# Attention feeding a gated layer on one core: fewer small attention matmuls, one batch's masks added elsewhere, and another order of the first phase

## The chip, the cores and the metric

One core of a Trainium2 chip runs the whole program. The core has five engines with queues of their own: TensorE (PE, with its weight loads shown as PEld), VectorE (DVE), ScalarE (ACT), GpSimd (POOL) and SyncE (SP, which issues the transfers). The metric is the device time of one execution in microseconds; less is better.

## What is computed

```python
scores = scale * np.matmul(q, k.transpose(0, 1, 3, 2))          # 8 batches, 8 heads, 576 x 64
mask_local = (rel >= 0) & (rel < 32)                            # heads 0 to 3
mask_strided = (rel >= 0) & (pos[None, :] % 32 == pos[:, None] % 32)   # heads 4 to 7
scores = np.where(masks[None, :, :, :], scores, -1000000000.0)
attn = softmax(scores)                                          # written out in full, 1e-09 in the sum
x = (attn @ v) as 4608 tokens x 512
out = (sigmoid(x @ w_gate) * (x @ w_val)) @ w_out               # 512 -> 1536 -> 512
```

All in 32-bit floats. The large products are made with the operands split in a rounded part and a remainder, three matmuls of 128x512 for each product.

## The kernel before

**Attention.** A batch has four *pairs* of heads: 0 and 2 are local, 1 and 3 are strided. A local pair works in 18 blocks of 32 queries, which see 64 keys each; a strided pair in 11 groups of 54 (three classes of the stride, 18 tokens each). One pair goes through these steps, named by letters in the order table: Q and V load, S makes the scores in PSUM (`score`), F0 adds the mask (`mask`), F1 takes the maximum, F2 or F3 subtracts it on VectorE or GpSimd, E is the exponential on ScalarE, N0 to N4 the sum, its reciprocal and the multiplication, T transposes the probabilities on TensorE and P copies them out of PSUM on ScalarE (in batches 3 to 7 VectorE transposes them instead, steps B), X multiplies by the values (`weigh`), H, L and R split the result. So `S32` is the scores of batch 3, pair 2.

`score` places the blocks in slots of 128 rows: four local blocks or two strided groups fill a slot, so 20 local and 12 strided places are computed for 18 and 11 blocks; the rest repeats the first blocks and is not used. Each place takes two matmuls (one for each head of the pair). In the batches of `BY_MASK` (0, 1 and 2) the mask is not added by VectorE: two matmuls of an identity with the mask (`masks`, 128x320 or 128x324) put it in PSUM first, and the scores accumulate onto it. F0 is then not there, and F1 and F2 read PSUM.

`weigh` takes the probabilities of a block from one half of the 128 rows (64 rows each, r = 0 or 1) and has 36 matmuls for a local pair. In batches 3 to 7 two blocks follow each other in one half, then two in the other; the last two blocks, 16 and 17, are both in half 0.

**The layer.** The first phase works on batch 0 alone: twelve chunks of the hidden dimension, each with its weights loaded as raw words (W), put together and split by ScalarE, VectorE and GpSimd (a, b, w, k, u, l, U, D), twelve matmuls for the gate and twelve for the value (g), and twelve for the output (O). The other batches follow in four steps of two batches (the last of one) with a scheme of seven products for a 2x2 block matrix; these matmuls are the lines 637.

**The order.** Nothing is scheduled by a planner: the table `ORDERS` lists all steps, one string for each part of the program, and each engine gets its instructions in that order. `|` is the next product of the current part. Engines run their queues in order, and wait on semaphores for what they read and for buffers to come free. The tiles in PSUM that the first phase's attention uses are few: `BANKS` gives them, and T of pair 1 and S of pair 3 in batch 0 have the same one (`"T01": "o0"`, `"S03": "o0"`).

Of the kernel before, what the change touches and what calls it, by code (L numbers as in the profile page):

```python
# [20 lines left out]
P = 128  # L21
# [3 lines left out]
LB = 32  # L25
# [21 lines left out]
BY_MASK = (0, 1, 2)  # L47
# [35 lines left out]
C Q00 Z00 W0.0 i0 a0.0 d4 Z01 b0.0 S00 F100 W0.1 F200 w0.0 p0.0 d7 E00 a0.1 Q01 N000 b0.1 S01 N100 W1.0 u0.0 N400 Q02  # L83
a1.0 N300 d1 T00 w0.1 p0.1 l0.0 F101 U0.1 F201 P00 E01 b1.0 V00 w1.0 S02 X00 Z02 R00 H00 N001 W0.2 N101 F102 a0.2 N401
F202 L00 W1.1 p1.0 V01 E02 N301 D0.1 d3 T01 b0.2 a1.1 g0.1.0 W2.1 N002 P01 U1.0 g0.0.0 l1.0 Q03 b1.1 X01 N102 S03 w1.1
N402 N302 W2.0 H01 a2.0 L01 p1.1 U1.1 Z03 T02 R01 F103 V02 g0.0.1 g0.1.1 F203 P02 b2.0 E03 g1.0.0 W2.2 w2.0 a2.1 X02
D1.1 g1.0.1 N003 N103 H02 p2.0 g1.1.0 u2.0 N403 N303 V03 w0.2 g1.1.1 T03 L02 Q11 W3.0 a2.2 g1.1.2 b2.2 g0.0.2 W1.2
k0.2 b2.1 R02 P03 Z30 w2.1 U0.2 X03 g1.0.2 w2.2 p2.1 D0.2 H03 g0.1.2 L03 a3.0 h0 b3.0 w3.0 R03 U2.1 a1.2 b1.2 g0.0.3
D2.0 g1.1.3 w1.2 s0 k1.2 k2.2 Z11 S11 W3.1 i1 u1.2 g0.1.3 k3.0 m0 W4.0 a4.0 g1.0.3 Q10 F111 g2.0 U2.2 U3.0 s1 F211 V11
l2.1 W4.1 h1 x0 h2 y0 W3.2 Z10 S10 m1 D1.2 E11 g2.1 l2.2 a3.1 K0 N011 N111 b3.1 D3.0 F110 O0 Z20 s2 a3.2 b4.0 N411 x1  # L90
N311 F210 T11 z0 w3.1 k3.1 y1 g3.0 V10 b3.2 m2 z2 Q12 w3.2 Q13 U3.1 E10 k3.2 l3.1 P11 W4.2 X11 U3.2 x2 w4.0 R11 N010
N110 h3 H11 O1 W5.1 S13 W5.0 a4.1 b4.1 Z13 N410 D3.2 k4.0 z1 w4.1 s3 N210 W5.2 k4.1 a4.2 y2 Z12 u4.0 F113 b4.2 U4.1
F213 a5.0 g3.1 T10 D4.0 b5.0 w4.2 a5.1 b5.1 k4.2 g4.0 P10 l4.1 U4.2 w5.0 m3 z3 S12 W6.0 O2 k5.0 l4.2 h4 E13 w5.1 s4
U5.0 a5.2 x3 b5.2 l5.0 F112 F212 X10 W6.1 w5.2 E12 Q21 k5.2 k5.1 a6.1 y3 R10 u5.2 W6.2 W7.0 g4.1 b6.1 w6.1 N012 h5 H10
# [1239 lines left out]
```

## Time and profile before

| what | value |
|---|---|
| time, median of 3 runs | 894.06 us (893.12 to 899.36) |
| the profiled execution | 893.55 us |
| its span, first to last instruction | 891.8 us |
| TensorE busy, share | 883.2 us, 99% |
| VectorE, ScalarE, GpSimd busy | 648.6, 473.3, 324.0 us |
| granted clock of TensorE | 1.000 |

A timeline lists merged instructions with start and length in us, the tiles they write and read, and the count. One fp32 matmul of the program leaves two records in the trace, one with rounded operands leaves one. TensorE's instructions overlap, so the cost of a block is read from its start to the next block's start.

### The profile page before, as it was taken

Reading aid. Unit: us, or ns where it says so; the run is one execution under the profiler, and the core shown is the slowest. Engines: PE = TensorE matmul, PEld = TensorE weight load, DVE = VectorE, ACT = ScalarE, POOL = GpSimd, SP = SyncE. Lnnn points to the kernel's source line nnn. Section 1 sums busy time; section 2 is a strip of 40 time slices with the busy share of each in tenths; the row PEclk is TensorE's granted clock in tenths of the full one; section 3 lists DMA queues with packets and bytes.
Section 4 is the critical chain, followed back from the end, with each engine's and each line's share of the span. In section 5 each row is a group of like instructions: output and inputs, shape, how many; then the busy total and the mean of one; then the engine's idle time right before and its main releaser. Section 6 shows DMA issues by size and latency. Waiting matters only on the chain.

```text
span 891.8 us, 18880 instructions
## 1 busy us (share of the span) xinstructions
PE 883.2 (99%) x7522; PEld 724.2 (81%) x7522; DVE 648.6 (73%) x993; ACT 473.3 (53%) x870; POOL 324.0 (36%) x259
## 2 busy tenths in 40 slices
PE   8999999999999999999999999999999999999997
PEld 6788888888888787888888888888888888888886
DVE  5898878999689999764789997233689852233874
ACT  5798767865566554544355535332646443233542
POOL 5553556965331575100034441001326420001194
PEclk9999999999999999999999999999999999999999
DMA  9998685895786799865536779775256896551577
GB/s 358 337 349 289 234 265 203 292 411 172 322 354 198 260 273 320 320 258 223 212 104 218 242 251 294 277 274 205 100 188 205 247 317 251 216 198 48 173 203 167
DMA packets 106120, 219.08 MB, mean 246 GB/s; under 512 B 44721, under 2 KB 64305, under 8 KB 99889
## 3 DMA queue, kind: packets, MB, share of 16 engines
q1 hardware_dynamic: 101712, 216.83, 70.5%
q10 hardware_dynamic: 4320, 1.05, 0.6%
q8 instruction: 59, 0.97, 0.4%
q14 instruction: 29, 0.23, 0.1%
HBM read 169.62 MB, written 48.23 MB: 244 GB/s over the span
## 4 chain that ended last, share of the span: by engine, by line
PE 91%; DVE 5%; DMA 1%; issue 1%; ACT 0%; POOL 0%; ACTq 0%; SPq 0%; DVEq 0%; POOLq 0%
PE sum L637 51%; PE g__2109 L637 11%; PE v__2110 L637 11%; PE sum L689 4%; PE v L637 4%; PE g L637 4%; PE s L382 3%; PE x L487 2%; DVE pt L457 1%; DMA qk<-in_qk_l 1%; PE t L444 1%; PE sum L487 1%; PE gv L637 1%; DVE stage L962 0%; DVE mx L424 0%
## 5 line engine op out<-in xcount | busy, mean ns | idle before, releaser
L637 PE MATMUL sum<-stage 128*128 128x512 f32 (+1 forms) x720 | 164.9, 386 | 0.7 <-ACT early_base L1044 0.7
L962 POOL TENSOR_TENSOR stage<-h,stage 128x512 fp32r<-128x512 f32 x67 | 100.0, 1514 | 180.2 <-ACT stage L960 148.9
L637 PEld LDWEIGHTS sum<-stage 128*128 128x128 f32 x720 | 132.0, 188 | 28.1 <-ACT early_base L1044 0.9
L960 ACT CAST stage<-h 128x512 fp32r<-128x512 f32 x168 | 97.5, 621 | 104.9 <-PE sum L637 30.8
L637 PE MATMUL sum<-x,mix 128*128 128x512 f32 x576 | 135.7, 390 | 0.2 <-ACT gq L837 0.2
L637 PEld LDWEIGHTS sum<-x,mix 128*128 128x128 f32 x576 | 107.8, 188 | 23.2 <-ACT gq L837 0.7
L457 DVE STREAM_TRANSPOSE pt<-sb 32x320 f32<-32x320 f32 (+1 forms) x160 | 85.7, 536 | 7.2 <-PE x L487 3.7
L825 DVE TENSOR_TENSOR s<-sum,gp 128x512 f32<-128x512 f32 x48 | 32.9, 688 | 74.4 <-PE sum L637 72.0
L962 DVE TENSOR_TENSOR stage<-h,stage 128x512 fp32r<-128x512 f32 x101 | 78.4, 800 | 8.3 <-ACT stage L960 6.8
L637 PE MATMUL sum<-x1h,mix 128*128 128x512 f32 x192 | 63.7, 391 | 0.0
L637 PE MATMUL sum<-x3h,mix 128*128 128x512 f32 x192 | 63.6, 391 | 0.0
L637 PE MATMUL sum<-x6h,mix 128*128 128x512 f32 x192 | 63.4, 390 | 0.0
L826 DVE TENSOR_TENSOR h<-s 128x512 f32<-128x512 f32 x48 | 35.4, 742 | 37.8 <-ACT s L827 37.4
L837 ACT COPY gq<-sum 128x512 f32<-128x512 f32 x48 | 28.1, 588 | 44.6 <-PE sum L637 44.5
L967 POOL TENSOR_TENSOR h<-h 128x512 f32<-128x512 f32 x13 | 18.7, 1436 | 86.2 <-DVE h L826 82.2
L827 ACT ACTIVATE s<-sum 128x512 f32<-128x512 f32 x24 | 14.3, 596 | 67.2 <-PE sum L637 67.2
L436 POOL TENSOR_TENSOR sb<-sb,mx 128x640 f32<-128x640 f32 (+1 forms) x15 | 20.8, 1390 | 75.0 <-DVE mx L432 67.5
L827 ACT ACTIVATE s<-s 128x512 f32<-128x512 f32 x48 | 30.0, 633 | 27.2 <-DVE s L825 27.2
L637 PEld LDWEIGHTS sum<-x3h,mix 128*128 128x128 f32 x192 | 36.0, 188 | 7.7
L637 PEld LDWEIGHTS sum<-x1h,mix 128*128 128x128 f32 x192 | 36.0, 188 | 7.7
L637 PEld LDWEIGHTS sum<-x6h,mix 128*128 128x128 f32 x192 | 36.0, 188 | 7.5
L825 DVE TENSOR_TENSOR s<-sum,gq 128x512 f32<-128x512 f32 x48 | 32.6, 685 | 10.8 <-PE sum L637 6.5
(237 smaller groups left out, 1947.8 us busy)
## 6 DMA issues: line engine op xcount, KB each, us to landing
mix<-mix SPq DMA_DIRECT2D x36, 1024.0 KB, 8.6
mix<-mix SPq DMA_DIRECT2D x36, 768.0 KB, 7.0
stage<-sums_out SPq DMA_DIRECT2D x96, 256.0 KB, 4.3
mix<-mix SPq DMA_DIRECT2D x12, 1792.0 KB, 8.4
stage<-outer SPq DMA_DIRECT2D x72, 256.0 KB, 4.1
vv<-in_v_l SPq DMA_DIRECT2D x16, 640.0 KB, 6.1
qk<-in_qk_l SPq DMA_DIRECT2D x16, 592.0 KB, 5.7
out<-turned_P SPq DMA_DIRECT2D x50, 128.0 KB, 4.0
```

The source lines that it names most:

```text
L382: nc.tensor.matmul(sc[g * m : (g + 1) * m, j * BANK + s * kk : j * BANK + (s + 1) * kk], qk[d, q0 : q0 + m], qk[d, k0 : k0 + kk], start=no ...
L436: engine.tensor_tensor(prob, prob, by_row, op=ALU.mult)
L457: nc.vector.transpose(dst[to : to + LB, :, col : col + LB], src[rows : rows + LB, :, h * LB : (h + 1) * LB])
L487: nc.tensor.matmul(halves[r][j * D : (j + 1) * D, (u * per + g) * m : (u * per + g + 1) * m], v[rows, (u * per + g) * P + j * D : (u * per ...
L637: nc.tensor.matmul(o, w, x, start=first and n == 0, stop=last and n == len(todo) - 1, skip_group_check=onto)
L689: nc.tensor.matmul(o, a[:, i * P : (i + 1) * P], b, start=first and n == 0, stop=last and n == 2)
L825: add = lambda to, x, y: nc.vector.tensor_tensor(to, x, y, op=ALU.add)
L826: mul = lambda to, x, y: nc.vector.tensor_tensor(to, x, y, op=ALU.mult)
L827: sig = lambda to, x: nc.scalar.activation(to, x, AF.Sigmoid)
L837: P6=(g2, v2, dict(P6=lambda: nc.scalar.copy(new("gq"), g2)), dict(P6=lambda: nc.scalar.copy(new("vq"), v2)), False),
L960: nc.scalar.copy(h, src)
L962: engine.tensor_tensor(l, src, h.bitcast(F32), op=ALU.subtract)
```

## The change

The scores of the batches in `BY_MASK` leave out the places that no block needs. Batch 2 leaves `BY_MASK`: its masks are added by VectorE, and its padded places stay. In local pairs of batches 3 to 7 block 17 goes to half 1 of the rows, in the scores, in the values' layout (made on the host, a zero block put ahead of it) and in `weigh`; the copy of the last 64 tokens then reads two pieces of 32 columns. `ORDERS` is written anew up to the first third of its second string.

```diff
-BY_MASK = (0, 1, 2)
+BY_MASK = (0, 1)
...
+        apart_last = local and b >= BY_PE
...
-            for n in range(ns * (P // m)):
+            blocks = NBL if local else NG
+            for n in range(blocks if by_mask else ns * (P // m)):
                 s, g = divmod(n, P // m)
-                q = n % (NBL if local else NG)
+                q = n % blocks
+                if apart_last and s == ns - 1:
+                    g = (g % 2) * 2 + g // 2
...
                 u, r = divmod(s, 2)
+                if apart_last and n == NBL - 1:
+                    r, g = 1, 0
...
-                left = [(halves[0][:, full : full + REST], lambda x: x)]
+                if not apart_last:
+                    left = [(halves[0][:, full : full + REST], lambda x: x)]
+                elif apart:
+                    left = [(halves[r][:, full : full + LB], lambda x, r=r: x[:, r * LB : (r + 1) * LB]) for r in range(2)]
+                else:
+                    src = xp.rearrange("p (r n) -> p r n", r=2)[:, :, full : full + LB]
+                    left = [(src, lambda x: x.rearrange("p (r n) -> p r n", r=2))]
...
-C Q00 Z00 W0.0 i0 a0.0 d4 Z01 b0.0 S00 F100 W0.1 F200 w0.0 p0.0 d7 E00 a0.1 Q01 N000 b0.1 S01 N100 W1.0 u0.0 N400 Q02
+Z01 C d4 Q00 i0 W0.0 a0.0 S00 b0.0 Z00 W0.1 F100 F200 w0.0 E00 N000 Z02 d7 a0.1 Q01 b0.1 S01 p0.0 u0.0 N100 N400 W1.0
...
```

What the new order does is seen on the engines. The lines of the changed kernel stand some 2 to 13 further down: its L370, L387, L449 and L453, L494, L650 and L702 are L368 (masks), L382 (scores), L444 and L448 (T), L487 (`weigh`), L637 and L689 (the layer's products) of before; its L402 and L406 are L397 and L401 (F0), L413 is L408 (F1), L421 is L416 (F2).

TensorE in batch 0, before, from the scores of pair 2 (`s_2`) on; `t_1` is T of pair 1, `x_1` its output, `v_0` and `g_0` the first chunk's products:

```order
L368 MATMUL s_2_261<-rounded 128x320 x2
L382 MATMUL s_2_261<-qk_2_234 32x64 x40
L487 MATMUL x_0_304<-pt_0_253,vv_0_258 64x32 x36
L680 MATMUL zeros_out<-zeros 128x256 x3
L444 MATMUL t_1_364<-cst,first_x_134 128x128 x6
L637 MATMUL v_0_373<-x_0_108,w_231 128x512 x3
L637 MATMUL g_0_383<-x_0_108,w_231 128x512 x3
L487 MATMUL x_1_390<-first_x_135 64x54 x22
L368 MATMUL s_3_414<-rounded 128x324 x2
L382 MATMUL s_3_414<-first_x_134 64x54 x24
L444 MATMUL t_2_455<-cst,sb_2_341 128x128 x4
L448 MATMUL t_2_455<-cst,sb_2_341 64x64 x2
```

The same place after the change:

```order
L370 MATMUL s_2_249<-rounded 128x320 x2
L387 MATMUL s_2_249<-qk_2_231 32x64 x36
L494 MATMUL x_0_300<-pt_0_245,vv_0_288 64x32 x36
L693 MATMUL zeros_out<-zeros 128x256 x3
L449 MATMUL t_1_356<-cst,first_x_115 128x128 x6
L650 MATMUL v_0_374<-x_0_108,w_224 128x512 x3
L370 MATMUL s_3_385<-rounded 128x324 x2
L387 MATMUL s_3_385<-first_x_115 64x54 x22
L494 MATMUL x_1_410<-first_x_116 64x54 x22
L449 MATMUL t_2_438<-cst,sb_2_184 128x128 x4
L453 MATMUL t_2_438<-cst,sb_2_184 64x64 x2
L650 MATMUL g_0_458<-x_0_108,w_224 128x512 x3
```

The masks and scores of pair 3 (`s_3`) now stand ahead of `x_1` and right behind the first three products; the second three (`g_0`) come behind `t_2`.

ScalarE beside it, before: the copies of `t_1` out of PSUM are the two L465, and L591 and L595 take the upper and lower words of a raw weight tile:

```order
L595 ACTIVATE first_x2h<-first_x0h 128x512
L535 COPY xr_117<-x_0_304 128x64
L527 CAST x_0_108<-x_0_304 128x512
L591 ACTIVATE first_x3l<-first_x1h 128x512
L420 ACTIVATE sb_2_341<-sb_2_341 128x640
L595 ACTIVATE first_x3l<-first_x1h 128x512
L591 ACTIVATE first_x3h<-first_x0l 128x512
L465 COPY first_x_135<-t_1_364 128x512
L465 COPY first_x_135<-t_1_364 128x256
L595 ACTIVATE first_x3h<-first_x0l 128x512
L527 CAST x_2_110<-x_1_390 128x16x18
```

After the change (L548 is the copy of the rest, L540 the rounding, L604, L608, L425 and L470 are L591, L595, L420 and L465):

```order
L608 ACTIVATE first_x2h<-first_x0h 128x512
L604 ACTIVATE first_x3l<-first_x1h 128x512
L548 COPY xr_114<-x_0_300 128x64
L540 CAST x_0_108<-x_0_300 128x512
L608 ACTIVATE first_x3l<-first_x1h 128x512
L604 ACTIVATE first_x3h<-first_x0l 128x512
L425 ACTIVATE sb_2_184<-sb_2_184 128x640
L608 ACTIVATE first_x3h<-first_x0l 128x512
L470 COPY first_x_116<-t_1_356 128x512
L470 COPY first_x_116<-t_1_356 128x256
L540 CAST x_2_110<-x_1_410 128x16x18
```

One L604 went ahead of the copy of `x_0`, and one L608 more stands ahead of the copies of `t_1`.

TensorE in batch 2, before, from the masks of pair 1 to the transposes of pair 0:

```order
L368 MATMUL s_1_1430<-rounded 128x324 x2
L382 MATMUL s_1_1430<-first_x_134 64x54 x24
L637 MATMUL v_7_1461<-x_0_108,w_1282 128x512 x3
L637 MATMUL v_7_1461<-x_1_109,w_1282 128x512 x3
L637 MATMUL v_7_1461<-x_2_110,w_1282 128x512 x3
L637 MATMUL v_7_1461<-x_3_111,w_1282 128x512 x3
L689 MATMUL sum_783<-w_1060,first_x6l 128x512 x3
L689 MATMUL sum_784<-w_1060,first_x6l 128x512 x3
L689 MATMUL sum_785<-w_1060,first_x6l 128x512 x3
L689 MATMUL sum_786<-w_1060,first_x6l 128x512 x3
L444 MATMUL t_0_1491<-cst,sb_0_801 128x128 x4
L448 MATMUL t_0_1491<-cst,sb_0_801 64x64 x2
```

After the change:

```order
L387 MATMUL s_1_1397<-first_x_115 64x54 x24
L650 MATMUL v_7_1424<-x_0_108,w_1326 128x512 x3
L650 MATMUL v_7_1424<-x_1_109,w_1326 128x512 x3
L650 MATMUL v_7_1424<-x_2_110,w_1326 128x512 x3
L650 MATMUL v_7_1424<-x_3_111,w_1326 128x512 x3
L449 MATMUL t_0_1454<-cst,sb_0_455 128x128 x4
L453 MATMUL t_0_1454<-cst,sb_0_455 64x64 x2
```

The masks are gone, and the transposes of pair 0 (`t_0`) come 12 products after the scores of pair 1, where there were 24.

## Rows read from the trace of the kernel before

**Rows 1.** Page, part 1: busy time of each engine, share of the span, instructions.

```profile
PE 883.2 (99%) x7522; PEld 724.2 (81%) x7522; DVE 648.6 (73%) x993; ACT 473.3 (53%) x870; POOL 324.0 (36%) x259
```

**Rows 2.** Waits of PE: who waited for whom, us in total, times, longest.

```profile
PE s L368 <- ACT pt L467: 0.8, 1, 0.8
...
PE t L444 <- POOL first_x L436: 0.5, 1, 0.5
PE s L382 <- DMA qk<-in_qk_l: 0.5, 1, 0.5
```

**Rows 3.** Timeline of PE, masks and scores: start, us, line, tiles, records.

```profile
84.96 0.46 PE L368 MATMUL s<-rounded 128*128 128x320 f32 x2
85.35 1.04 PE L382 MATMUL s<-qk 64*32 64x64 f32 x80
86.32 3.06 PE L637 MATMUL g<-x,w 128*128 128x512 f32 x12
...
155.02 0.39 PE L637 MATMUL v__2110<-x0l,mix 128*128 128x512 f32 x1
155.25 0.39 PE L637 MATMUL v__2110<-x0h,mix 128*128 128x512 f32 x1
155.56 1.04 PE L382 MATMUL s<-qk 64*32 64x64 f32 x80
```

**Rows 4.** PE in stretches of one local output block: us, busy (records under way).

```profile
216.91:217.14 0.23, 0.23 (x16) 1.00 0.00 0
...
217.85:218.08 0.23, 0.23 (x24) 1.00 0.73 280
218.08:218.20 0.12, 0.12 (x8) 1.00 1.09 444
```

**Rows 5.** Timeline of PE, batch 0, pairs 1 to 3.

```profile
18.50 0.87 PE L444 MATMUL t<-cst,first_x 128*128 128x128 f32 x6 [0.47 <-POOL first_x L436]
19.13 0.95 PE L637 MATMUL v<-x,w 128*128 128x512 f32 x3
...
20.70 0.91 PE L487 MATMUL x<-first_x 54*64 54x54 f32 x44
21.54 0.57 PE L368 MATMUL s<-rounded 128*128 128x324 f32 x2
22.04 0.92 PE L382 MATMUL s<-first_x 64*64 64x54 f32 x48
22.89 0.66 PE L444 MATMUL t<-cst,sb 128*128 128x128 f32 x4
```

**Rows 6.** Timeline of ACT beside it.

```profile
16.62 0.21 ACT L535 COPY xr<-x 128x64 f32<-128x64 f32 x1 [1.89 <-PE x L487]
...
19.09 0.68 ACT L591 ACTIVATE first_x3h<-first_x0l 128x512 f32<-128x512 f32 x1
19.68 0.82 ACT L465 COPY first_x<-t 128x512 f32<-128x512 f32 x2
```

**Rows 7.** VectorE's mask additions and subtractions: busy us, mean ns, idle before.

```profile
L401 DVE TENSOR_TENSOR sb<-s,cst 128x324 f32<-128x324 f32 x20 | 8.9, 484 | 3.4 <-PE s L382 3.3
...
L397 DVE TENSOR_TENSOR sb<-s,cst 128x640 f32<-128x640 f32 x10 | 8.1, 811 | 2.4 <-PE s L382 2.4
...
L416 DVE TENSOR_TENSOR sb<-sb,mx 128x640 f32<-128x640 f32 x7 | 7.1, 1015 | 0.1
...
L416 DVE TENSOR_TENSOR sb<-s,mx 128x640 f32<-128x640 f32 x6 | 4.9, 818 | 0.1
```

**Rows 8.** Busy us by engine in two stretches (PE, PEld, DVE, ACT, POOL).

```profile
80.00:160.00 80.00, 80.00 (x993) 64.81 (x992) 65.22 (x94) 60.36 (x115) 43.93 (x36) 1.00 0.68 233
160.00:220.00 60.00, 59.75 (x373) 48.87 (x372) 58.43 (x87) 40.38 (x69) 42.74 (x39) 1.00 0.77 302
```

**Rows 9.** Timeline of DVE, a local pair of batch 2: maximum to reciprocal.

```profile
88.10 0.82 DVE L408 TENSOR_REDUCE mx<-s 128x10 f32<-128x640 f32 x1
...
97.56 0.22 DVE L432 RECIPROCAL mx<-mx 128x10 f32<-128x10 f32 x1
```

More of the change, by code (lines that the diff above doesn't have):

```diff
@@ L185 @@
[L185 to L186 removed]
+Z01 C d4 Q00 i0 W0.0 a0.0 S00 b0.0 Z00 W0.1 F100 F200 w0.0 E00 N000 Z02 d7 a0.1 Q01 b0.1 S01 p0.0 u0.0 N100 N400 W1.0
+w0.1 Q02 a1.0 F101 F201 N300 T00 P00 d1 S02 V00 E01 b1.0 p0.1 W0.2 W1.1 Q03 w1.0 a0.2 l0.0 X00 Z12 U0.1 N001 R00 d3
+N101 F102 p1.0 N401 H00 V01 N301 b0.2 T01 F202 U1.0 a1.1 E02 L00 Z03 D0.1 W2.1 b1.1 W2.0 g0.1.0 N002 N102 N402 V02 P01
@@ new lines @@
+@j0.14.0.1 K3 | B41.3 E42 @j0.15.1.1 R40 @g0.16.1 | @g0.16.0 =C.1.P5 V41 | @G0.18 H40 @j0.16.0.1 N042 @G0.19 B41.2
+@O0.P2 B41.6 @j0.16.1.0 Z43 @G0.20 @g0.17.0 N142 | @i0.17.1 @g0.17.1 Q50 F043 | N442 =C.1.P7 @i0.18.0 X41 F143
+@g0.18.1 =C.0.P7 | R41 @g0.18.0 @A1.0.0 V42 @i0.17.0 @i0.19.1 @j0.17.1.0 @g0.19.1 @i0.18.1 @j0.18.0.0 @A1.0.1 |
+@T4.4.1 @j0.17.0.0 | @j0.18.1.0 @J1.h0 F243 N342 B42.0 B42.2 | @g0.20.0 B42.4 B42.3 @i0.19.0 Z50 | B42.7 @g0.19.0
+@g0.20.1 B42.5 H41 @i0.20.0 @A1.1.0 @J1.L0 | E43 N043 @L0.0.0 | @j0.19.0.1 B42.1 B42.6 N143 @L0.1.0 @i0.20.1
@@ new lines @@
+@j0.19.1.0 X42 @j0.20.0.1 N443 N343 =C.0.P7t =C.0.P3 | B43.0 B43.1 H42 V43 @A1.1.1 @j0.20.1.1 | | @J1.T1 @L0.1.1 B43.6
+@J1.h2 B43.4 B43.3 B43.5 @J1.h1 | @L0.0.1 @A1.2.1 B43.2 R42
+""",
+    """
+| B43.7 X43 | @J1.L1 H43 =C.0.P4 =C.1.P3 =C.1.P4 R43 =A0.1.P1 @J1.T2 @J1.h3 @L1.0.0 S50 | =A0.0.P1 @J1.l2 @J1.l3
+@J1.T3 | @J1.h4 @J1.T4 | @J1.h5 F050 Z51 K4 @O0.P4 =A0.0.P6 | =C.1.P7t =C.0.P3t Q51 F150 | @J1.l4 @J1.L5 @J1.h6
+=A0.1.P6 | F350 =A0.0.P5 =A0.1.P5 | E50 =C.1.P3t S51 =A0.0.P7 @J1.l6 @L1.1.0 N050 @O0.P7 @O0.P3 | F051 =A0.s22 F151
@@ L187 @@
+@i1.19.1 H62 @g1.19.0 @j1.16.1.0 @j1.17.0.0 S70 @i1.18.0 @A2.0.1 N463 | @j1.18.1.0 @g1.18.0 =C.0.P7 @J2.T1 | @i1.20.1
+N363 @A2.1.0 | Z72 @A2.1.1 @g1.19.1 V63 | B63.0 @O1.P2 B63.7 =C.0.P7t @i1.19.0 @i1.20.0 @j1.18.0.0 B63.2 @j1.19.0.1
+B63.6 @J2.h1 | | @g1.20.1 @g1.20.0 =C.0.P3 B63.1 @j1.19.1.0 =C.1.P7t @j1.20.0.1 @j1.20.1.1 F070 B63.4 @A2.2.1 =C.1.P3
+R62 B63.3 @L0.0.0 B63.5 F170 @A2.2.0 @J2.l1 @L0.1.0 | | @A2.3.0 | X63 @L0.0.1 @L0.1.1 @A2.3.1 @J2.h2 H63 =C.0.P4 R63
+@J2.T2 |
 """,
@@ L1289, in stacked, with by_batch @@
         return a.reshape(-1, 2, P, a.shape[4] * per * P)
-    def by_batch(a, per, n):
-        return np.concatenate([stacked(a[FEW], per)[..., :n], stacked(a[MOST], per // 2)[..., :n]], 0)
+    def by_batch(few, most, per, n):
+        return np.concatenate([stacked(few, per)[..., :n], stacked(most, per // 2)[..., :n]], 0)
     keys = np.arange(NBL)[:, None] * LB + np.arange(KL)[None, :]
-    v_l = by_batch(np.concatenate([lead, vl], 2)[:, :, keys], LG, VL * P)
-    v_s = by_batch(grouped(vs), 2, SS * P)
+    v_l = np.concatenate([lead, vl], 2)[:, :, keys]
+    last = NBL - 1
+    parted = np.concatenate([v_l[:, :, :last], np.zeros_like(v_l[:, :, :1]), v_l[:, :, last:]], 2)
+    v_l = by_batch(v_l[FEW], parted[MOST], LG, VL * P)
+    v_s = grouped(vs)
+    v_s = by_batch(v_s[FEW], v_s[MOST], 2, SS * P)
     wg, wv = (w.reshape(NC, P, NF, P).transpose(2, 1, 0, 3).reshape(NF, P, 512) for w in (w_gate, w_val))
```

186 lines of the change are left out of this document (85 added, 101 removed).

## The prediction

> **What bounds the kernel now.** I read the page's busy times first: TensorE is busy 99% of the span [rows 1]. The page warns that a busy TensorE need not be at its peak, so the list of its waits came next. Its largest are 0.8, 0.5 and 0.5 us [rows 2], one time each, and all of them lie in the first 20 us, where attention of batch 0 is a chain of dependent steps and little else is there to do. After that TensorE goes from block to block. So the time is TensorE's own work plus a few waits at the start; an edit counts by the TensorE time that it takes away, and by waits that it adds. Idle time of other engines is worth nothing. I therefore read every block from its start to the start of the next one in TensorE's timeline.
>
> **Masks of batch 2.** Four pairs lose their two mask matmuls. The pair at 84.96 us takes 0.39 us until the scores begin [rows 3]. Not all of it comes back: with no mask ahead, the last product before the scores of 155.56 takes 0.31 us where the one before it takes 0.23 [rows 3], so 0.08 moves to it. That is 0.31 us a pair and 1.24 us for four; the bounds are 1.2 and, if nothing moves, 1.6.
>
> **Padded places in batches 0 and 1.** Forty local score matmuls take 0.97 us (85.35 to 86.32, [rows 3]), 24 ns each; four fewer are worth 0.10. Twenty-four strided ones take 0.85 us (22.04 to 22.89, [rows 5]), 35 ns each; two fewer are worth 0.07. Four pairs of either kind make 0.68 us. The lower bound is nothing, if the last matmuls run beside others anyway.
>
> **Block 17 in the other half.** Ten local pairs (batches 3 to 7) have it. In the output block at 216.91 us, 16 records begin in the first 0.23 us: 8 matmuls, 29 ns each. In the last but one stretch 24 are under way, of which 16 had begun before, and in the last stretch only 8, with none new [rows 4]: the last four matmuls began at half the pace, 58 ns each. These are blocks 16 and 17, both in half 0, while half 1 has nothing left. If block 17 runs in half 1 beside block 16, they go at 29 ns: up to 0.12 us a pair. As the second half can start only behind the first in the queue, I take 0.08, and 0.8 us for ten pairs; bounds 0 and 1.2. The Trainium skill (TensorEngine Tiling (Array Packing), Key Properties) says that different tiles load and multiply in parallel, which would be four here, two halves of the rows by two halves of the columns. By that the fullest tile goes from ten matmuls to nine, 0.06 us a pair and 0.6 in all, and the whole block would last about 0.6 us; the timeline's block of 1.29 us [rows 4] disagrees, so the 0.8 stands. The copy that is now two pieces is ScalarE's, which nothing waits for here.
>
> **Sum on TensorE:** 1.24 + 0.68 + 0.8 = 2.7 us.
>
> **The new order at the start.** Up to the transposes of pair 1 (18.50 us) both orders make the same chain, and the shorter first scores bring it forward by 0.10: 18.40. Then they part. Before, six products follow, then `x_1`, then masks and scores of pair 3 at 21.54 [rows 5]. Now three products follow, to 18.40 + 0.63 + 0.79 = 19.8, and the masks of pair 3 stand next. They write the tile in PSUM from which ScalarE copies `t_1`. Those copies began at 19.68 and took 0.82 [rows 6]. In the new order one instruction of the 0.59 that passes from 19.09 to 19.68 has left the row ahead of them and one like it has come in; the one that went ahead of the copy of `x_0` (16.62) can hold it up by nothing to 0.6, and I take 0.3. The copies then end at 20.8 (20.5 to 21.1), and TensorE waits 1.0 us (0.7 to 1.3), with everything in its queue behind it. From there: masks 0.50, scores 0.85 - 0.07, `x_1` 0.84 [rows 5], so the transposes of pair 2 come at 22.9, as before (22.89), but with three products fewer done, and three are worth half of the 1.57 us from 19.13 to 20.70: 0.8 us lost. The savings in batch 0's scores (half of 0.68) are used up in this walk: the chain, not the matmuls, sets the time there.
>
> **VectorE.** Batch 2 adds two additions of 0.81 and four of 0.48 us, and two subtractions now read the sum in SBUF, 1.02 us each where those from PSUM take 0.82 [rows 7]: 3.6 + 0.4 = 4.0 us. I cost it at nothing: VectorE has 14.8 us idle from 80 to 160 us [rows 8]. Without that cover it is the first rival.
>
> **Total:** 893.55 - (2.7 - 0.34) + 0.8 = 892.0 us on the scale of the profiled execution, whose span of 891.8 leaves 1.75 us around it. The median of the runs is 0.5 above the profiled one, so I give **892.2 us**.
>
> **Rivals.** *VectorE becomes late in batch 2 (ends on the other side).* From the maximum of a local pair's scores to the reciprocal VectorE needs 9.7 us (88.10 to 97.78, [rows 9]), with other work between. The addition makes it 10.5, and GpSimd's multiplication follows before TensorE can transpose. The transposes of pair 0 now stand 12 products after pair 1's scores, where there were 24, so 12 products, 2.7 us, of room are gone. From 160 to 220 us VectorE is busy 58.4 of 60 us [rows 8], so what is late there is not made up. If all 4.0 us come through, the time is 896.2. Against it stand the 14.8 us. It decides against me once more than 1.6 us of the 4.0 pass through. The Trainium skill (GPSIMD Engine Reference, Key points) has a rule that speaks for it: GpSimd shares its SBUF interfaces with VectorE and collides with VectorE's instructions that have two inputs in SBUF, and the subtraction becomes one of those. The two subtractions' means agree with it.
>
> *The wait at the scores of pair 3 does not come, and the start gets shorter.* If the copies of `t_1` end by the time the three products do, the 0.8 us are not lost, and if half of the 1.8 us of waits goes too, the time is 892.2 - 0.8 - 0.9 = 890.5. For it: only one ScalarE instruction stands between. Against: in the row ScalarE works from 16.62 to 20.50 with hardly a pause, so the copies cannot be much earlier than 20.5.
>
> *The edits on TensorE bring nothing but the masks.* If the padded places and block 17 ran beside other matmuls already, 1.24 are left and the start takes 0.8 of them: 893.3. For it: the records of one block overlap. Against: the halved pace at the end [rows 4].
>
> **How the numbers follow.** Forecast, 0.45: 892.2, with its terms' bounds 891.0 to 893.4. VectorE or another wait of the new order passes through, 0.23: 893.5 to 896.5. Shorter start, 0.15: 889.5 to 891. Only the masks, 0.12: 893.0 to 893.8. Something worse, 0.05: a wait that repeats over the first phase, above 897. The range 889.5 to 896.5 holds about 0.9 of this before the spread of the runs themselves, whose median lies 0.5 above the profiled one; the runs' highest is far above and I take it for no guide. About 1% (9 us) is what a measurement of this kernel can tell from no change. Faster by that needs 885, below what the sum and all three waits together give (893.55 - 2.7 - 1.8 = 889.0): 0.02. Slower needs 903, over 10 us of new waits: 0.03. The same: 0.95.
>
> **What will show it.** TensorE: no mask matmuls past batch 1, 36 and 22 scores in batches 0 and 1, and local output blocks of about 1.20 us in batches 3 to 7 where they were 1.29. A new wait of about 1 us at the masks of pair 3 of batch 0, released by ScalarE's copy. VectorE's busy time up by about 4 us, and the transposes of batch 2 without a wait. I am wrong on the size if the waits on VectorE and GpSimd between 75 and 220 us grow past 1 us in all, or if TensorE's start-to-start times of the small blocks do not shrink; and wrong in kind if the time moves by more than 5 us either way.

## The result, and the profile of the changed kernel

The changed kernel takes 901.43 us (median; 899.8 to 903.27), the kernel before 894.1 in the same session: a ratio of 1.0084, 95% interval 1.007 to 1.0098. It is slower by 0.8%, 7.3 us, outside the predicted 889.5 to 896.5. The profiled execution took 903.27; its span is 901.5 us against 891.8 [rows 1], and the difference, 9.7 us, is what is accounted for below. That execution is the longest of the six, 1.8 us above their median, so the 9.7 us hold something of its own: most of all the late load at the start, the second wait below. In the experiments one execution of e4 (1459.5 us, granted clock 0.557) is left out of its ratio; it lifts the median of its ten from 899.15 to 899.58.

The page, part 1 and the clock's row of part 2 (to be laid beside [rows 1]):

```profile
span 901.5 us, 18789 instructions
PE 884.9 (98%) x7466; PEld 723.3 (80%) x7466; DVE 659.0 (73%) x999; ACT 468.3 (52%) x872; POOL 324.9 (36%) x259
PEclk9999999999999998999999999999999999999999
```

TensorE has 56 records fewer and yet is busy 1.7 us longer; one slice of its clock reads 8. VectorE is busy 10.4 us longer, where four were counted; most of the rest are instructions stretched beside GpSimd's, of which more below (all that VectorE's instructions took beyond the median of those that met none of GpSimd's is 73.5 us, 66.6 before). The waits of PE (who waited for whom, us in total, times, longest), beside [rows 2]:

```profile
PE g__2083 L494 <- issue: 3.6, 1, 3.6
PE s L387 <- DMA first_x<-in_qk_s: 2.0, 1, 2.0
PE x L494 <- issue: 1.3, 1, 1.3
...
PE s L370 <- ACT first_x L470: 0.7, 1, 0.7
...
PE sum L650 <- DVE stage L975: 0.4, 1, 0.4
PE v__2084 L650 <- DMA mix<-mix: 0.3, 1, 0.3
```

The first and the third are new, and neither lies at the start; the second, at 12.22 us, is a load of the start. Line 494 is the value products: g__2083 those of batch 4 pair 2 (at 343.37 us), x those of batch 3 pair 3 (at 299.83).

Where the 9.7 us came in is read off the start of every 512-column product, of which both kernels have 3,420 in one sequence. How much later the n-th begins than in the kernel before:

```
product no.     0      30     420    960    1050   1080   1140   1230   1890   2730   end
at (before)   19.13  32.53  148.9  281.3  305.5  312.3  330.1  354.7  521.6  721.3   span
later by, us   1.39   2.51   1.95   1.72   3.22   4.45   4.03  10.35   9.99  10.63   9.7
```

Four stretches: the start (1.4, then 2.5, and 3.25 at product 120, of which batch 2's missing masks bring 1.2 back by product 390); 281 to 330 us (2.3, with waits of 0.33, 1.30 and 0.35); 330 to 355 us (6.3); and a small one by 721 us (0.64). Some 1.2 us of the 4.45 at product 1080 are no loss: the new order has 80 scores ahead of that product which the old one has behind it, and at product 1140 both have done the same. The last 0.9 come back at the end, where the kernel before waits 0.7 us for a staged sum. From 355 to 700 us the lag shrinks by some 0.08 at each local output block: that is the block 17 edit at work. The two stretches from 160 to 220 us and before, where the prediction looked for VectorE, stay full of TensorE (busy us of PE, PEld, DVE, ACT, POOL, clock; compare [rows 8]), and behind the long wait there is a stretch at half clock:

```profile
80.00:160.00 80.00, 80.00 (x992) 64.10 (x991) 68.24 (x102) 59.56 (x116) 43.55 (x37) 1.00 0.71 250
160.00:220.00 60.00, 59.81 (x373) 48.74 (x371) 58.39 (x83) 39.44 (x69) 43.01 (x37) 1.00 0.77 293
...
320.00:343.37 23.37, 19.80 (x239) 15.95 (x237) 22.98 (x35) 10.18 (x24) 15.24 (x11) 0.99 0.95 301
343.37:349.53 6.16, 6.16 (x81) 5.32 (x82) 5.74 (x11) 2.49 (x4) 2.52 (x2) 0.50 0.46 152
```

Ahead of the long wait VectorE is busy 22.98 of 23.37 us. In the clock's record the half clock lasts 6.83 us, from 342.70, so it costs TensorE some 3.1 us (half of the 6.16 behind 343.37). Wait and clock make 6.7, about the jump in the table.

What the wait of 3.57 us is for. PE's timeline, then VectorE's, then GpSimd's (start and length, us):

```profile
337.82 1.98 PE L650 MATMUL sum<-stage 128*128 128x512 f32 x8
343.37 0.32 PE L494 MATMUL g__2083<-pt,vv 64*64 64x32 f32 x2 [3.57 <-issue]
```

```profile
334.16 2.89 DVE L975 TENSOR_TENSOR stage<-h,stage 128x512 fp32r<-128x512 f32 x1
336.97 1.91 DVE L421 TENSOR_TENSOR sb<-sb,mx 128x648 f32<-128x648 f32 x1
338.80 3.07 DVE L462 STREAM_TRANSPOSE pt<-sb 32x320 f32<-32x320 f32 x6
341.91 0.83 DVE L429 TENSOR_REDUCE mx<-sb 128x12 f32<-128x648 f32 x1
342.77 0.50 DVE L462 STREAM_TRANSPOSE pt<-sb 32x320 f32<-32x320 f32 x1
```

```profile
333.84 2.66 POOL L584 TENSOR_TENSOR x0l<-raw,x0h 128x1024 fp32r<-128x1024 f32 x1 [1.87 <-DMA stage<-outer]
336.46 3.57 POOL L975 TENSOR_TENSOR stage<-h,stage 128x512 fp32r<-128x512 f32 x2
```

The value products need the transposes of pair 2 (L462). The last that they begin with starts at 342.77 and takes 0.50; they begin 0.1 us behind its end. "Issue" only says that the profile shows no releaser. In VectorE's queue stand ahead of it: pair 3's row sum (341.91), and two instructions that took 2.89 and 1.91 us, where their like have 0.68 and 0.83 elsewhere (medians of those that met none of GpSimd's). Both began while GpSimd was at work and ended 0.55 and 0.69 us after its instruction: 336.50 to 337.05, and 338.19 to 338.88 (of the x2 row the first ends at 338.19).

### The profile page after: what moved, and what is told of

Read it like the earlier page. It is cut to its first block, busy times and chain, and to the rows that moved or that the text cites. A ratio compares the mean times of both kernels' runs of the same rounds, so it can differ in the third digit from the quotient of the medians.

```text
span 901.5 us, 18789 instructions
## 1 busy us (share of the span) xinstructions
PE 884.9 (98%) x7466; PEld 723.3 (80%) x7466; DVE 659.0 (73%) x999; ACT 468.3 (52%) x872; POOL 324.9 (36%) x259
## 4 chain that ended last, share of the span: by engine, by line
PE 82%; DVE 7%; DMA 4%; ACT 2%; issue 2%; POOL 2%; SPq 0%; DVEq 0%; ACTq 0%
PE sum L650 46%; PE v__2084 L650 10%; PE g__2083 L650 10%; PE sum L702 4%; PE v L650 3%; PE g L650 3%; PE s L387 2%; PE x L494 2%; DMA first_x1h<-in_w_all 2%; DVE stage L975 1%; DVE pt L462 1%; DMA mix<-mix 1%; DMA stage<-sums_out 1%; DVE mix L795 1%; PE sum L494 1%
## 5 line engine op out<-in xcount | busy, mean ns | idle before, releaser
L650 PE MATMUL sum<-stage 128*128 128x512 f32 (+1 forms) x720 | 166.9, 389 | 0.4 <-DVE stage L975 0.4
L650 PEld LDWEIGHTS sum<-stage 128*128 128x128 f32 x720 | 133.1, 190 | 28.3 <-DVE stage L975 1.2
L650 PE MATMUL sum<-x,mix 128*128 128x512 f32 x576 | 135.2, 390 | 0.0
L650 PEld LDWEIGHTS sum<-x,mix 128*128 128x128 f32 x576 | 107.9, 188 | 22.4
L462 DVE STREAM_TRANSPOSE pt<-sb 32x320 f32<-32x320 f32 (+1 forms) x160 | 85.7, 536 | 8.5 <-PE x L494 4.6
L975 DVE TENSOR_TENSOR stage<-h,stage 128x512 fp32r<-128x512 f32 x101 | 80.8, 824 | 6.0 <-ACT stage L973 4.8
L650 PE MATMUL sum<-x6h,mix 128*128 128x512 f32 x192 | 63.7, 391 | 0.2 <-DVE s L838 0.2
L650 PE MATMUL sum<-x3h,mix 128*128 128x512 f32 x192 | 63.7, 392 | 0.0
L650 PE MATMUL sum<-x1h,mix 128*128 128x512 f32 x192 | 63.4, 390 | 0.0
L650 PEld LDWEIGHTS sum<-x6h,mix 128*128 128x128 f32 x192 | 36.0, 188 | 8.4 <-DVE s L838 0.9
L650 PEld LDWEIGHTS sum<-x3h,mix 128*128 128x128 f32 x192 | 36.0, 188 | 7.8
L650 PEld LDWEIGHTS sum<-x1h,mix 128*128 128x128 f32 x192 | 36.0, 188 | 7.6
```

Of the source, the lines that this page charges most:

```text
L462: nc.vector.transpose(dst[to : to + LB, :, col : col + LB], src[rows : rows + LB, :, h * LB : (h + 1) * LB])
L650: nc.tensor.matmul(o, w, x, start=first and n == 0, stop=last and n == len(todo) - 1, skip_group_check=onto)
L975: engine.tensor_tensor(l, src, h.bitcast(F32), op=ALU.subtract)
```

## Experiments

Theories: LATE ORDER, the new order of 285 to 345 us makes the loss. VECTORE, batch 2's added masks make VectorE late. START, the new order's first steps. PORT and QUEUE are two forms of LATE ORDER: VectorE's instructions stretched beside GpSimd's, or simply too many ahead of the transposes. FETCH, TensorE short of its own instructions. In every diff tokens of the order stand in the order in which they are executed; a token is one step.

### Code or order

The code alone: the changed functions, the old order, and four steps for batch 2's masks.

```
-... g6.1 u7.2 F120 F220 k8.0 ...
+... g6.1 u7.2 F020 F120 F220 k8.0 ...      (F021, F022, F023 likewise)
```

> The changed code (masks of batch 2 on VectorE, trimmed scores, block 17 in the other half) in the order of the kernel before; the adds of batch 2's masks stand right ahead of the row maxima of the same pair. Theory LATE ORDER (what was lost was lost in the new order of 285 to 345 us: the wait of 3.6 us of batch 4 pair 2's value products, its clock fall, and the wait of 1.3 us of batch 3 pair 3's): none of these waits is there, TensorE saves 2.0 to 2.7 us, time 891 to 892.5. Theory VECTORE (batch 2's 4 us of adds make VectorE late, and the waits of 285 to 345 us are that lateness arriving): the waits come in this order too, time 895 or more. Theory START (the load and first steps of the new order cost 1.4 to 2): as LATE ORDER here.

The order alone. Batch 2's maxima and subtractions (F12., F22.) stand where the new order has the additions, since the scores' bank is free only behind them.

```
-BY_MASK = (0, 1)        and the new code
+BY_MASK = (0, 1, 2)     and the old code
-... S21 g7.1 Z31 ... F021 T20 ... F121 ... F221 ... S23 ...
+... S21 g7.1 ... F121 F221 T20 ... S23 Z31 ...
```

> The code of the kernel before (masks of batch 2 as products of TensorE, padded scores, block 17 where it was) in the new order; as batch 2's adds aren't there, its maxima and subtractions stand in their places, and one clearing of a buffer (pair 1 of batch 3) comes later, behind the last scores of batch 2. LATE ORDER: all of the loss and none of the saving, 903 to 905, with a wait of 3 us or more at batch 4 pair 2's value products and a stretch at half clock behind it. VECTORE: VectorE has 4 us less to do, the waits at 285 to 345 us shrink to under 1 us each, 895 to 897. START: its 1.4 to 2 us are in either.

Measured: code alone 894.07 against 893.79 (ratio 1.000, 0.998 to 1.0019); order alone 902.63 (1.0094, 1.0064 to 1.0123). The order carries the loss: without any mask addition on VectorE it has the same wait at the same step (3.58 us) and the same 6.83 us at half clock. VECTORE falls for that wait. It doesn't for the small one: at batch 3 pair 3 e2 waits 0.31 us, the changed kernel, e3, e5, e6 and e8, which have the code too, 1.28 to 1.30, though VectorE's long instruction there is the same (1.74 us in e2); what of the code makes the difference is open. And LATE ORDER's other half is wrong too: the code alone saves nothing where 2.0 to 2.7 us were expected. That is taken up below.

### Which part of the order

New order up to the value products of batch 3 pair 3 (near 300 us), old order from there; and the reverse. Both with the changed code.

```
e3:  new: Z01 C d4 Q00 ... X33  | old: every step not yet done, in the old sequence
e4:  old: C Q00 Z00 W0.0 ... X33  | new: every step not yet done, in the new sequence
```

> The changed code; the new order up to the value products of batch 3 pair 3 (near 300 us), and from there the order of the kernel before. LATE ORDER: the 3.6 us wait and the half clock are gone, what the start and batch 3 pair 3's wait lost stays (the lag near 300 us was 3.2 us): 896 to 898. VECTORE: lateness has been made by then and comes out at batch 4 in any order: 900 or more.

> The changed code; the order of the kernel before up to the same place near 300 us, from there the new one. LATE ORDER: batch 4 pair 2's wait of 3 us or more and the half clock behind it are there, start and batch 3 pair 3 are as before: 897 to 900. If the lateness is handed on from the first phase instead (by the order there or by VECTORE's adds), batch 4 pair 2 waits under 1 us and the time is under 894.

Measured: 897.20 (1.003, 1.0011 to 1.0048) and 899.58 (1.0064, 1.004 to 1.0088). The part behind 300 us makes the larger loss by itself: with the old order in front the wait is again 3.58 us, the half clock again 6.83. The part in front costs about 3 us by itself (897.20 against e1's 894.07). In e4 the first product began at 20.75 us, later than in any other profile, though its start is the old one; with the new start it began at 19.0 (e2), 19.36 (e3) and 20.52 (the changed kernel), with the old one at 18.91 in e1. The load of the 2.0 us wait above landed at 12.18 us in the changed kernel and between 9.25 and 10.63 in the 13 other profiles, six of which have the new start too. So that wait comes with the execution, not with the order alone.

### Is it the steps, or VectorE's queue?

```
e5, the changed kernel, "|" being a group of TensorE's products:
-... @j0.19.1.0 X42 @j0.20.0.1 N443 N343 =C.0.P7t =C.0.P3 | B43.0
+... @j0.19.1.0 @j0.20.0.1 N443 N343 =C.0.P7t =C.0.P3 | X42 B43.0
e6, the changed kernel:
-... B42.5 H41 @i0.20.0 @A1.1.0 @J1.L0 | E43 N043 @L0.0.0 | @j0.19.0.1 B42.1 B42.6 N143
+... B42.5 B42.1 B42.6 H41 @i0.20.0 @A1.1.0 @J1.L0 | E43 N043 @L0.0.0 | @j0.19.0.1 N143
```

> The changed kernel whole, with one step moved: the value products of batch 4 pair 2 stand behind the next group of products of TensorE instead of ahead of it. LATE ORDER: the group fills most of the wait of 3.57 us, no stretch at half clock follows (its 6.8 us cost 3.1), so 5 to 6 us come back: 895.5 to 897. If the wait only moves with the step (VectorE is as late wherever the products stand), a wait of over 2.5 us remains and the time is 900 or more.

> The changed kernel whole, with two of VectorE's transposes for batch 4 pair 2 moved ahead of pair 3's exponential and row sum. If these two steps' place alone made the wait: it falls from 3.57 us to about 2.7 (the row sum of 0.83 us that stood ahead of them is passed), and to under 1.5 if more stood ahead than the row sum. LATE ORDER in its queue form (VectorE as a whole is 3 us late there): 2.5 to 2.9 us of wait and the half clock remain, 899.5 to 901.

Measured: e5 903.02 (1.01, 1.0081 to 1.012), e6 899.85 (1.0065, 1.0048 to 1.0082). With the value products out of the way, the next group meets the same lateness:

```profile
PE sum L647 <- DVE stage L972: 3.8, 2, 3.5
```

So moving that step by a group of products doesn't help, and LATE ORDER's 895.5 to 897 is missed: VectorE as a whole is late, and its next result is as late. In e6 the wait is 2.10 us, between what was expected if the row sum alone stood in the way (2.7) and if more did (under 1.5); the clock falls for 3.41 us, half as long as behind 3.57 (us, PE busy, the others, clock):

```profile
343.52:346.93 3.41, 3.41 (x10) 2.64 (x9) 3.06 (x5) 0.81 (x1) 2.51 (x2) 0.50 0.91 333
```

### What makes VectorE late: GpSimd's step beside it

The diff moves one step of GpSimd, x0l (@J1.L0, L584, a subtraction of 1,024 columns that makes the low part of a mixed input), from behind the value products X42 to ahead of pair 3's exponential. e8 puts it back in the changed kernel, e9 brings it forward in the kernel before.

```
e8: -... @A1.1.0 @J1.L0 | E43 N043 ... X42 @j0.20.0.1
    +... @A1.1.0 | E43 N043 ... X42 @J1.L0 @j0.20.0.1
e9: -... N043 B42.1 B42.6 ... X42 ... R42 B43.5 @J1.L0 B43.2
    +... N043 @J1.L0 B42.1 B42.6 ... X42 ... R42 B43.5 B43.2
```

> The changed kernel whole, with one step of GpSimd moved: the low half of superblock 1's first mixed input (x0l, 2.66 us at 333.84 in the changed kernel) is issued behind the value products of batch 4 pair 2 instead of ahead of the exponential of pair 3; the kernel before has it there, at 338.0. Theory PORT (two VectorE instructions, 2.89 us instead of 0.68 and 1.91 instead of 0.83, began just behind a GpSimd instruction and ended 0.55 to 0.7 us after it: they waited for GpSimd): both take under 1 us, 3.3 us of VectorE's queue are given back, the wait of 3.57 us at the value products falls under 1 us, no half clock, 896 to 898.5. Theory QUEUE (VectorE is late there because the new order puts more in front of the transposes, whatever GpSimd does): the wait stays over 2.5 us and the time over 900.

> The kernel before, code and order, with that one step of GpSimd moved up to where the changed kernel has it: behind the row maxima's reciprocal chain of batch 4 pair 3's start (its row sum), ahead of three of GpSimd's own steps on the staged sums. PORT: VectorE instructions that read two operands from SBUF and begin just behind it last until its end, some 2 us are lost there, the wait at batch 4 pair 2's value products grows from 0.2 to 1 to 2.5 us, 895 to 898. QUEUE: GpSimd has room there and nothing changes, 893.5 to 894.3.

Measured: e8 898.21 (1.006, 1.0046 to 1.0074), e9 896.76 (1.0029, 1.0019 to 1.0038). One step of GpSimd, moved either way, moves the time by 2 to 3 us, in the kernel before too, where it is the only edit: e9 is 3.1 us slower by the medians (2.6 by the ratio), and e8 is 3.2 us faster than the changed kernel by the medians of two sessions (2.1 by the ratios, whose intervals overlap a little). Part of e9's loss is clock: four of its nine executions have a mean granted clock of 0.997 or 0.998 and took 896.8 to 897.7 us, the five at 0.999 or 1.000 took 895.0 to 896.8, the profiled one among them. VectorE in e9, GpSimd beside it, and PE's wait:

```profile
328.24 2.85 DVE L960 TENSOR_TENSOR stage<-h,stage 128x512 fp32r<-128x512 f32 x1
```

```profile
328.14 2.40 POOL L569 TENSOR_TENSOR x0l<-raw,x0h 128x1024 fp32r<-128x1024 f32 x1
```

```profile
PE g__2109 L485 <- DVE pt L455: 1.6, 1, 1.6
```

VectorE began 0.10 us behind GpSimd and ended 0.55 us after it (331.09 against 330.54). In e8 the 2.89 us instruction is gone, the wait is 1.17 us and the clock stays full; the second long instruction is still there, beside another step of GpSimd:

```profile
331.31 2.48 DVE L972 TENSOR_TENSOR stage<-h,stage 128x512 fp32r<-128x512 f32 x4
333.71 1.93 DVE L418 TENSOR_TENSOR sb<-sb,mx 128x648 f32<-128x648 f32 x1
```

```profile
333.36 1.58 POOL L972 TENSOR_TENSOR stage<-h,stage 128x512 fp32r<-128x512 f32 x1 [2.44 <-ACT stage L970]
```

In the kernel before the same products wait 0.21 us, and x0l stands behind them:

```profile
336.15 0.25 PE L487 MATMUL g__2109<-pt,vv 64*64 64x32 f32 x2 [0.21 <-DVE pt L457]
```

```profile
338.00 2.40 POOL L571 TENSOR_TENSOR x0l<-raw,x0h 128x1024 fp32r<-128x1024 f32 x1
```

So PORT holds, and QUEUE, which expected no change from e9 and over 900 us from e8, falls. PORT's expectation for e8 is missed in part: the second instruction is still stretched, and 1.17 us of wait are left where under 1 was expected. That instruction lost 1.1 us, about as much; whether the rest of the wait would go with it wasn't tested.

### Where the code's own saving went

In e1's profiled execution (895.15 us; the median of its ten is 894.07) TensorE stood still twice in the middle of a run of like products, with every semaphore of its next instructions met. PE's timeline of the first, scores of batch 2 pair 0, and of the second, shortly behind value products:

```profile
84.69 0.84 PE L385 MATMUL s<-qk 64*32 64x64 f32 x62
86.67 0.41 PE L385 MATMUL s<-qk 64*32 64x64 f32 x18 [1.13 <-issue]
...
316.04 1.89 PE L648 MATMUL sum<-stage 128*128 128x512 f32 x7
319.93 1.32 PE L648 MATMUL sum<-stage 128*128 128x512 f32 x5 [2.00 <-issue]
```

The packets of the DMA queue that the page calls "q8 instruction" come 59 times, 16 KB each; in the trace of before TensorE and its weight loads run 256 instructions from one to the next on average (14,847 in 58 intervals), so they are TensorE's own. One such packet landed at 85.34 and one at 318.44, 1.3 and 1.5 us before the restarts; the second took 1.96 us where most take 1.0.

e7 spreads the small products over more time, by moving two steps; e11 makes the stream 96 instructions longer ahead of batch 2, by computing the padded scores again.

```
e7:  -... S20 x5 ... g6.0 b8.1 ...            +... x5 ... g6.0 S20 b8.1 ...
     -... X40 F142 K3 @j0.14.0.1 | ...        +... F142 K3 @j0.14.0.1 | X40 ...
e11: -for n in range(blocks if by_mask else ns * (P // m)):
     +for n in range(ns * (P // m)):
```

> The changed code in the order of the kernel before, as in the run with the code alone, with two steps moved: the scores of batch 2 pair 0 stand behind 12 more products of 512 columns, and the value products of batch 4 pair 0 behind the next group of products. In the run with the code alone TensorE stood still 1.13 us in the middle of those scores and 2.00 us shortly behind those value products, with every semaphore met, 1.3 and 1.5 us after a transfer of 16 KB of its own instructions had landed. Theory FETCH (its next instructions had not come, because small products used a block of them up faster than the next is brought): both stops are gone, TensorE keeps the saving of 2.0 to 2.7 us, 890.8 to 892. Rival (the stops are a lateness of operands that the trace doesn't show): stops of 1 us or more at the same steps, 893.5 to 894.5.

> The changed code without its middle part (the padded scores of batches 0 and 1 are computed as before) in the order of the kernel before. TensorE computes 0.3 us more than in the run with the code alone, and its stream is 96 instructions longer (24 products each in two batches, a weight load with each) before batch 2 begins. FETCH: a block of instructions now begins ahead of batch 2 pair 0's scores and of batch 4 pair 0's, not inside them, so the stops of 1.13 and 2.00 us are gone: 891.3 to 892.5, though it computes more. Rival (lateness of operands): both stops are there, 894.2 to 894.6.

Measured: e7 893.85 (0.9995, 0.9984 to 1.0006); e11 892.79 against 893.68 (0.9992, 0.9984 to 1.0001). The times don't decide: e7 lies in the rival's range, e11 just above FETCH's, and neither is clear of e1. The traces do. In e11, which computes more than e1, both stops are gone, and no semaphore was touched. In e7 the first is gone and the second 0.61 us, but two new waits came for it (0.69 for a staged sum's load at 293, 0.79 at value products at 345).

The place of the stops says the same, counted in records of TensorE and its weight loads from the start of the trace:

```
stop of            e1 1.13   e1 2.00   e7 0.61   e5 0.78   e8 1.41
at, us               86.67    319.93    318.22    357.68    353.52
records ahead        2,497     6,849     6,849     7,617     7,617
as 256 x n + 193      n= 9        26        26        29        29
packets landed           9        26        26        29        29
```

Each stop falls on the same place in a block of 256, and ends behind the landing of the packet of that number; the waits for VectorE's transposes fall elsewhere (remainders 67 and 19 in the changed kernel, 132 in e2, 14 in e4, where the stops have 193). So FETCH holds for these stops. What sets when such a packet is sent isn't settled: in e1 the second was sent 15 us after the one before it, and 509 of TensorE's records lay between.

One more wait takes from the code's saving, and it is VectorE's. In the four profiles of the changed code in the old order (e1, e4, e7, e11) the value products of batch 2 pair 2 wait 0.40 to 0.42 us near 144 us for ScalarE's copies, and in the kernel before they don't:

```profile
143.47 1.49 PE L492 MATMUL x<-pt,vv 64*64 64x32 f32 x72 [0.42 <-ACT pt L470]
```

In e11 the scores of pair 3 stand 1.06 us earlier than before (135.57 for 136.63), but VectorE's two added masks follow (0.90 us), ScalarE's exponential begins only 0.13 us earlier (139.22 for 139.35), and the copies stand behind it in ScalarE's queue.

Block 17 alone, in the kernel before (with the lines that set g and r for the last block, and the layout of v). It acts in ten local pairs, batches 3 to 7; the expectation names too few batches:

```
+        apart_last = local and b >= BY_PE
```

> The kernel before with the block 17 edit alone (batches 3 to 5, local pairs): masks, padded scores and order as before. TensorE saves 0.08 to 0.09 us in each of ten places that VectorE and GpSimd don't touch, and its instructions keep their number and so their places in the blocks that are brought. All theories: 892.9 to 893.2. If the next wait of TensorE takes it back at each place (a staged sum or a transpose that ends at the same time as before): 893.8.

Measured: 893.11 (0.9995, 0.9986 to 1.0004), as expected and not clear of no change. In the trace the lag falls by 0.05 to 0.09 at nine of the ten local output blocks; the tenth, at 335 us, waits for VectorE's transposes and gains nothing. Most comes back: 0.1 at a load near 293, 0.33 at the first product with the next superblock's mixed weights at 554, 0.08 near 695, so that 0.17 of 0.8 us are left from 149 us to the last product. In e11 0.8 of 1.0 us come back at the like place at 716, behind a load that took 7.2 us where the kernel before had 5.2; why it did is open.

### The new order mended

```
-... @A1.1.0 @J1.L0 | E43 ... X42 @j0.20.0.1      (as e8)
+... @A1.1.0 | E43 ... X42 @J1.L0 @j0.20.0.1
-... B33.1 ... @T3.3.0 @i0.8.1 ... B33.5 =C.0.P5 B33.2 @G0.13
+... B33.1 ... @i0.8.1 ... B33.5 =C.0.P5 B33.2 @T3.3.0 @G0.13
 and the padded scores as in e11
```

> The changed kernel in its new order with three repairs: x0l behind batch 4 pair 2's value products as in the run before last; one VectorE step of the forming of outputs (h, 1.75 us in the changed kernel at 296.80, begun 0.11 us behind a GpSimd step) moved behind the last two transposes of batch 3 pair 3; and the padded scores of batches 0 and 1 computed as in the kernel before, so that TensorE's stream is 96 instructions longer. PORT: the transposes end 1.7 us earlier, the wait of 1.30 us at batch 3 pair 3's value products falls under 0.3. FETCH: the stop of 1.41 us in the middle of batch 5's first scores (at 353.5, all semaphores met, 1.2 us after 16 KB of instructions had landed) is gone or under 0.5. Together 1.1 + 1.4 less 0.3 for the padding off the 898.2 of x0l alone: 895.7 to 896.7. If either reason is wrong its wait stays: 897 to 898.2. Against the kernel before the order's slower start (1.2 to 2 us) should be what is left.

The second line is the changed kernel's other wait, 1.30 us at 299.83. GpSimd, and VectorE beside it, in the changed kernel:

```profile
296.69 1.31 POOL L975 TENSOR_TENSOR stage<-h,stage 128x512 fp32r<-128x512 f32 x1
```

```profile
296.80 1.75 DVE L980 TENSOR_TENSOR h<-h 128x512 f32<-128x512 f32 x1
298.58 1.15 DVE L462 STREAM_TRANSPOSE pt<-sb 32x384 f32<-32x384 f32 x2
```

Measured: 895.85 (1.0022, 1.0013 to 1.0031), 2.15 us above the kernel before, where the changed kernel is 7.3 above it. The wait at 299.83 and the stop at 353.5 (1.41 us in e8) are gone. Of what is left, the waits at batch 4 pair 2's value products and at batch 0 pair 3's masks:

```profile
PE g__2107 L491 <- issue: 1.3, 1, 1.3
...
PE s L367 <- ACT first_x L467: 0.4, 1, 0.4
```

The best version is e11: old order, masks on VectorE, block 17 moved, scores padded. By the ratios it beats the changed kernel by 0.9%; the kernel before it doesn't beat measurably.

## Why the prediction was wrong

The measured time lies in the band above 897 that the prediction gave 0.05 (for a wait that repeats; none does), and moved by more than the 5 us at which it called itself wrong in kind; the interval of the result is 0.14% to either side, much less than the 1% that it took for the noise. By its own steps:

- **Masks of batch 2**, 1.24 us: right. In e11 the lag falls by 1.19 between products 180 and 390. The scores of batch 2 follow a product directly, beside [rows 3]:

```profile
87.64 0.61 PE L650 MATMUL g<-x,w 128*128 128x512 f32 x2
88.19 1.04 PE L387 MATMUL s<-qk 64*32 64x64 f32 x80
```

- **Padded places**, 0.68: right in sign, twice too large. Local scores took 0.968 us and take 0.900, strided ones 0.850 and 0.837: 4 x 0.068 + 4 x 0.013 = 0.33. The strided term was the wrong one (0.013 for 0.07).
- **Block 17**, 0.8 us: right in the blocks. The local output block took 1.285 us and takes 1.202, predicted 1.20, at eight of ten places. As a saving it is not shown: e10 kept 0.17 us of it in its trace.
- **Start**: the mechanism was right. The masks of batch 0 pair 3 wait for ScalarE's copies, as the prediction walked it from [rows 5, 6]: 0.66 us here and 0.27 to 1.03 in the other profiles of the new order, for 1.0 (PE, and ScalarE's copies that end at 22.07):

```profile
22.12 0.57 PE L370 MATMUL s<-rounded 128*128 128x324 f32 x2 [0.66 <-ACT first_x L470]
```

```profile
21.23 0.84 ACT L470 COPY first_x<-t 128x512 f32<-128x512 f32 x2
```

  The size is too small: in e2, whose first product was on time, the new order is 1.8 us late at product 120, where 0.8 and 0.34 were counted. Between products 0 and 120 TensorE waits 1.47 us there and not at all in the kernel before: 0.73 at these masks, and 0.16, 0.29 and 0.28 at 29, 35 and 48 us, behind the 22.9 us at which the walk ends.
- **VectorE's additions in batch 2**, nothing: right. From 80 to 160 us it is busy 3.0 us more [rows 8], and no wait follows in the new order; in the old one they cost the 0.4 us told above.
- **The sum** is the step that failed: "TensorE's own work and a few waits at its start". Its reading of [rows 2] passes over 1.0 us at the very start and 0.7 at 879 us, but between those no wait behind 20 us is over 0.25. It took this property of the old order over to an order that had been searched anew for hundreds of microseconds, and it walked only the first 25. The runs showed what stood outside every term: two new waits at 300 and 343 us (1.30 and 3.57), made by GpSimd's steps beside VectorE's, a clock fall (3.1) and, with the code alone, the lack of instructions (1.13 and 2.00). A rival for waits of the new order was there, but with one place (VectorE in batch 2, 160 to 220 us) and a price of up to 896.2 that came from lost room in front of one transpose, not from the place where VectorE had least room.
- The **forecast of a gain** failed twice over, then: the order lost some 9 us (e2), and the code kept at most 0.9 of 2.4, in e11 and not clear of noise.

The rival named the right mechanism at the wrong place. It rested on the Trainium skill, "GPSIMD Engine Reference", section "Key points": GpSimd shares its SBUF interfaces with VectorE, with contention for VectorE instructions in a two-port mode or with two SBUF inputs. The trace agrees, and shows which ones. In the trace of before 163 VectorE instructions with two operands (TENSOR_TENSOR) began while one of GpSimd's was running. Of the 67 that read an operand from PSUM, where TensorE's products land, none took over 0.25 us longer than its like elsewhere. Of the 96 with both operands in SBUF 69 did, and 68 of the 72 that had over 0.4 us of GpSimd's instruction still before them. Of the 437 that began otherwise one did, and of 137 transposes and reductions that began beside GpSimd none. So batch 2's subtraction did become one that can be stretched, as the rival says, and so are the two in front of the 3.57 us wait (h and stage, sb and mx). A stretched one of 128x512 ends 0.55 us (median) after GpSimd's instruction, so it loses what is left of that instruction, less 0.13: 2.2 us for x0l, 1.1 for a staged sum.

What in the trace of before would have shown it: for each GpSimd instruction that the order moves, which two-operand VectorE instruction begins in it, and which wait of TensorE has no slack behind that. In the kernel before the value products of batch 4 pair 2 wait 0.2 us, at 336.15, for their transposes, and x0l stands behind them, at 338.00.

## What to carry to other kernels

A kernel that keeps one engine 99% busy has no waits because its order has none; an order that is changed over hundreds of microseconds has to be walked that far, engine by engine, not only where the diff's purpose lies. Look first where the second engine is full (VectorE here, 98% from 320 to 343 us) and at long steps of GpSimd that move beside its two-operand work. And a saving of a few small products is not free of side effects either: it shifts the rest of the instruction stream and every later meeting of engines and loads.

## What the runs showed of the hardware

- The granted clock after a stop of TensorE: in the profiled executions it was 0.5 for 6.83 us behind stops of 3.57, 3.58, 3.58 and 3.51 us (the changed kernel, e2, e4, e5), for 3.41 us behind 2.10 (e6), and stayed at full behind 2.00 (e1) and less (1.57 in e9, 1.41 in e8). The fall came between 0.67 us ahead of TensorE's restart (the changed kernel) and 2.36 us behind it (e6). The two levels are 1.2 and 2.4 GHz. So a stop can cost more than itself: here 3.1 us on top of 3.57. It isn't the same in every execution: the mean granted clock of e2's six is 0.995 to 0.998.
- TensorE can stand still with all its operands there, because its instructions are not: 1.13 and 2.00 us in e1, 0.61 in e7, 0.78 in e5 and 1.41 in e8, each in or just behind small products (80 records of scores and their weight loads run in 0.97 us), at one place in a block of 256 instructions, and 1.2 to 1.5 us after a 16 KB packet of instructions landed.
- The loads of the start land at different times from one execution to the next: that of pair 1's queries and keys between 9.25 and 12.18 us in 14 profiles, and the first 512-column product began between 18.91 and 20.75 us (e1 and e4, which have the same start).
- A VectorE instruction with both operands in SBUF that begins beside a GpSimd instruction lasts until 0.55 us (median, 128x512) behind that instruction's end: 2.89 us for 0.68 in the changed kernel. One that reads an operand from PSUM doesn't (67 cases in the trace of before).
